# Two heads' transposed probabilities leave PSUM in one step, and q is loaded ahead of the values, in an attention and two feed-forward layers

## The chip, the cores and the metric

The kernel runs on one core of a Trainium2 chip. The metric is the device time of one execution in microseconds. The time before is the median of three runs.

## The reference

Windowed attention with a few global keys, then two feed-forward layers on its output:

```python
# q, k, v: (2, 8, 768, 64); n_global = 8, n_local = 96
scores = q @ k.T / sqrt(64) + bias            # ALiBi bias, per head
keep = is_global | ((rel >= 0) & (rel < n_local))
a = softmax(where(keep, scores, -1e9))
x = (a @ v) as (1536, 512)                    # tokens x (heads * 64)
h = x @ w_in;  x = maximum(0.01 * h, h) @ w_out          # w_in (512, 2048), w_out (2048, 512)
h = x @ w_in2; x = P(h) / (Q(h) + 1e-6) @ w_out2         # P cubic, Q quadratic in h
```

All inputs are float32. The kernel works with float32 products split into a high and a low part (three matmuls for one).

## The kernel before

**Attention.** The 16 combinations of batch and head are taken as 8 pairs of heads (`Pair`, numbered 0 to 7). A pair has 6 blocks of 128 queries (i = 0 to 5) and 2 heads (j), which makes 12 units. A unit is one block of queries of one head against its window of 256 keys (128 for i = 0). The code is written unit by unit along slots n = 0, 1, 2, ...; a pair has 12 slots, called s0 to s11 here. Each engine takes its instructions in the order of this text (`manual_schedule`), so the slot at which a step is written sets what it stands behind. A unit goes through these steps:

- `scores` (L376, TensorE): three matmuls into half a PSUM bank, the two heads interleaved. From n = 8 on, every fourth slot (s0, s4, s8) issues the scores of four units, which fill both halves of the two banks `sc0` and `sc1`. The next group needs both banks read.
- `least` (L387, VectorE): adds the bias, negates, finds the row's least. It is what frees a score bank. Before, it stands at s0, s2, s4, ... for two units each.
- `exp` (L401, ScalarE), one slot after the unit's number.
- `transposes` (L412, TensorE) into a tile `pt` of 256 columns, and `evacuate` into `pts` (L418 on ScalarE, L420 on VectorE), three slots after.
- `values` (L431 to L434, TensorE) into the bank `o`, `LV` = 5 slots after.
- `finish` (L440 to L443, VectorE) after three blocks of both heads: divides by the sum and writes `xp`. Before, it is written at s5 and s11.

**Fillers.** At the end of each slot stand pieces of other work, as generators that advance one step per slot:

- `prep_k` and `prep_q` of the next pair, in halves: three transposes on TensorE into one of two banks `h` (L305), a ScalarE copy one slot later (`kh`, L315, or `qt`, L348), and for k a VectorE step (`kl`, L317) one slot after that; then GpSimd steps. The slots are in the tables `PREP0` (during pair 0) and `PREP`. Here "k0, q0, k1, q1" are the halves.
- `x_out` of the pair before, in halves at s8 and s10 ("x0" and "x1"): transposes into a bank `h` (L198), ScalarE `xh` (L202), VectorE `xl` (L204). The second half's `xl` stands at s0 of the following pair, and q0 of that pair takes the bank which this `xl` frees.
- `decode` of a raw weight piece, started at s10 (the table `DECS`): a DMA of 512 KB into `wraw` (L126), then ScalarE "low" (L133), VectorE "sign" (L141), ScalarE "high" (L138), two GpSimd steps, ScalarE "hi" (L160), VectorE "lo" (L163), each in a slot of its own; "low" stands at s3 of the next pair, "lo" at s0 of the pair after it.
- Loads on SyncE's DMA queue: k two pairs ahead at s4 (`LOAD_K`), v one pair ahead at s6 (`LOAD_V`, six DMAs, L296 to L298), q two pairs ahead at s9 (`LOAD_Q`, L283). The raw tile `qr` has one buffer: the load of q for pair p+2 waits until q1 of pair p+1 has been transposed.

**Feed-forward.** 96 steps of 24 matmuls of 512 columns each, from about 119 us to the end.

Of the kernel before, what the change touches and what calls it, by code (L numbers as in the profile page):

```python
# [8 lines left out]
F32 = mybir.dt.float32  # L9
# [3 lines left out]
AF = mybir.ActivationFunctionType  # L13
# [4 lines left out]
P = 128  # L18
# [7 lines left out]
def attention_moe_moe2(  # L26
# [15 lines left out]
    nc = tc.nc  # L42
# [11 lines left out]


    PREP0 = (("prep_k", 2, 0), ("prep_q", 4, 0), ("prep_k", 6, 1), ("prep_q", 8, 1))
    PREP = (("prep_k", 0, 0), ("prep_q", 1, 0), ("prep_k", 4, 1), ("prep_q", 6, 1))
    LOAD_K = 4
    LOAD_V = 6
    LOAD_Q = 9  # L60
    XOUT = (8, 10)

    FIRST = 8
# [4 lines left out]
    DEC_WAIT = 4  # L68
    DECODE = (0, "low", "sign", "high", "shift", "join", 0, 0, "hi", 0, "lo")

    ON_ACT = (1, 2, 4, 5, 7, 8, 10)


    NF_EARLY = 5
# [116 lines left out]
    ident = cpool.tile([P, P], F32, name="ident")  # L191
# [15 lines left out]
    W2 = 2 * P  # L207
# [36 lines left out]
    def attention(wpool, w1, ffn):  # L244
        with ExitStack() as actx:
# [3 lines left out]
            upool = actx.enter_context(tc.tile_pool(name="upool", bufs=3))  # L249
            ps = actx.enter_context(tc.tile_pool(name="ps", bufs=2, space=PSUM))  # L250

            pairs = [(b, hp) for b in range(B) for hp in range(NPAIR)]
            PU = 2 * NB
# [102 lines left out]
            class Unit:  # L356
# [22 lines left out]
                def least(self):  # L379
                    i, w = self.i, self.w  # L380
                    if self.ih == 0 and self.j == 0:
                        self.pair.st[self.half] = upool.tile([P, 2, 2, HB], F32, tag="st", name="st")
                    self.st = self.pair.st[self.half]
                    self.least_at = self.st[:, 0, self.j, self.ih : self.ih + 1]
                    self.sn = upool.tile([P, W2], F32, tag="sn", name="sn")
                    b0 = W2 if i == 0 else 0
                    nc.vector.tensor_tensor_reduce(  # L387
                        self.sn[:, :w],
                        self.sc[:, :w],
                        bias[:, 2 * self.pair.hp + self.j, b0 : b0 + w],  # L390
                        -0.125,
                        3.0e38,
                        ALU.add,
                        ALU.min,
                        self.least_at,
                    )

                def exp(self):
                    w = self.w
                    self.pr = upool.tile([P, W2], F32, tag="pr", name="pr")  # L400
                    nc.scalar.activation(  # L401
                        self.pr[:, :w],
                        self.sn[:, :w],
                        AF.Exp,
                        bias=self.least_at,
                        scale=-1.0,
                    )

                def transposes(self):
                    self.pt = ps.tile([P, W2], F32, tag="pt", name="pt")  # L410
                    for c in range(0, self.w, P):
                        nc.tensor.transpose(self.pt[:, c : c + P], self.pr[:, c : c + P], ident)  # L412

                def evacuate(self):
                    w = self.w
                    self.pts = upool.tile([P, W2], F32, tag="pts", name="pts")
                    if self.on_act():
                        nc.scalar.activation(self.pts[:, :w], self.pt[:, :w], AF.Copy)  # L418
                    else:
                        nc.vector.tensor_copy(self.pts[:, :w], self.pt[:, :w])  # L420

                def on_act(self):
                    return self.n % PU in ON_ACT

                def values(self):
                    i, j, pr = self.i, self.j, self.pair
# [9 lines left out]
                def finish(self):  # L436
                    pr, st, o = self.pair, self.st, self.pair.o[self.half]
                    if self.half == 0:
                        pr.xp = apool.tile([P, NB, P], F32, tag="xp", name="xp")
                    nc.vector.tensor_scalar(st[:, 1], o[:, :, :, D], 1e-9, None, ALU.add)  # L440
                    nc.vector.reciprocal(st[:, 1], st[:, 1])
                    xp = pr.xp[:, self.half * HB : (self.half + 1) * HB]
                    nc.vector.tensor_tensor(  # L443
                        xp.rearrange("p i (j d) -> p j i d", j=2),
                        o[:, :, :, 0:D],
                        st[:, 1].unsqueeze(3).to_broadcast([P, 2, HB, D]),
                        ALU.mult,
                    )

            P_ = [Pair(n) for n in range(len(pairs))]  # L450
            for p in P_:
                p.st, p.o = {}, {}
            U = [Unit(n) for n in range(PU * len(pairs))]
# [51 lines left out]
            def fillers(n):  # L505

                p, s = divmod(n, PU)
                for g in list(running):
                    if next(g, running) is running:
                        running.remove(g)  # L510
                new = []
                if p + 1 < len(P_):
                    nxt = P_[p + 1]
                    for what, slot, half in PREP0 if p == 0 else PREP:
                        if s == slot:
                            new.append(getattr(nxt, what)(half))
                    if s == LOAD_V:
                        nxt.load_v()
                    if s == LOAD_K and p + 2 < len(P_):
                        P_[p + 2].load_k()  # L520
                    if s == LOAD_Q and p + 2 < len(P_):
                        P_[p + 2].load_q()
                if 0 < p < len(P_):
                    for half, slot in enumerate(XOUT):
                        if s == slot:
                            new.append(P_[p - 1].x_out(half))
                if p == 0 and s in BIAS:
                    bias_head(2 + BIAS.index(s))
                if n in DECS and early:
                    new.append(decode(*early.pop(0)))  # L530
                if n == PU:
                    load_coef()
                if n == 2 * PU:
                    prepare_coef()
                if n == H_SLOT:
                    new.append(ffn.head(0))
                if n == 0:
                    start(k1)
                    start(q1)
                for g in new:  # L540
                    start(g)

            def unit(n):
                return U[n] if 0 <= n < len(U) else None

            LV = 5
            GROUPS = {m: (m,) for m in range(0, FIRST, 2)}
            GROUPS.update({m: (m, m + 2) for m in range(FIRST, len(U), 4)})
            n = 0
            while n < len(U) or running or n <= len(U) + LV + 1:  # L550

                for m in GROUPS.get(n, ()):
                    for _ in zip(unit(m).scores(), unit(m + 1).scores()):
                        pass
                if n % 2 == 0 and unit(n):
                    unit(n).least()
                    if n == 0:
                        bias_head(1)
                    unit(n + 1).least()
                if unit(n - 1):  # L560
                    unit(n - 1).exp()
                if unit(n - 3):
                    unit(n - 3).transposes()
                    unit(n - 3).evacuate()
                if unit(n - LV):
                    unit(n - LV).values()
                if unit(n - LV - 1) and unit(n - LV - 1).ih == HB - 1 and unit(n - LV - 1).j == 1:
                    unit(n - LV - 1).finish()
                fillers(n)
                n += 1  # L570
# [426 lines left out]
    with ExitStack() as fast:  # L997
        fast.enter_context(tc.manual_schedule())
        wpool = fast.enter_context(tc.tile_pool(name="wpool", bufs=1))
        dram = fast.enter_context(tc.tile_pool(name="dram", bufs=1, space=bass.MemoryType.DRAM))  # L1000
        scratch = [dram.tile([P, 2 * DM], F32, name=f"scratch{f}") for f in range(NF)]
        last_xp = dram.tile([P, NB, P], F32, name="last_xp")
        w1 = []
        ffn = Layers(fast, w1)
        attention(wpool, w1, ffn)
        ffn.run(wpool, True, AHEAD)
# [44 lines left out]
```

## Time and profile before

| what | value |
|---|---|
| time before, median of 3 runs | 648.39 us (647.54 to 649.64) |
| profiled execution, its own time | 648.33 us |
| span from its first to its last instruction | 646.5 us |
| TensorE busy | 629.3 us (97%) |
| VectorE, ScalarE, GpSimd busy | 473.0, 440.7, 208.8 us |
| first score matmul of pair 0, pair 1, pair 2, pair 7 | 7.39, 23.59, 36.41, 101.52 us |

Matmuls are pipelined, so TensorE counts as busy while it waits for less than a matmul's own length. Where it waits is read from the starts of its instructions, not from the busy share. A pair lasts from the first score matmul of its s0 to that of the next pair.

### The profile page before, as it was taken

How to read it: one execution, taken by the hardware profiler on the slowest of the kernel's cores; microseconds unless marked ns; L12 is line 12 of the kernel's file. 1: busy time of each engine (PE TensorE's matmuls, PEld its weight loads, DVE VectorE, ACT ScalarE, POOL GpSimd, SP SyncE). 2: the span in 40 equal slices, each digit the busy share in tenths (PEclk: the TensorE clock that was granted, in tenths of full speed). 3: DMA queues.
4: the chain of work that ended last, by engine and by line, in shares of the span. 5: the costliest groups of instructions: out<-in, count | busy, mean ns of one | idle time of the engine just before them, and what ended most of it. 6: DMA issues, size and time to landing. Idle time of an engine off the chain costs nothing.

```text
span 646.5 us, 9591 instructions
## 1 busy us (share of the span) xinstructions
PE 629.3 (97%) x3264; PEld 528.2 (82%) x3264; DVE 473.0 (73%) x933; ACT 440.7 (68%) x829; POOL 208.8 (32%) x220
## 2 busy tenths in 40 slices
PE   5999999999999999999999999999999999999996
PEld 4888888888888888888888888888888888888884
DVE  6788888787896655656444469998777777897785
ACT  4788888777875654546444467776677888876672
POOL 3777675444444343433000002222222222112220
PEclk9999999999999999999999999999999999999999
DMA  8677553653458767676322310000013333000001
GB/s 186 147 175 168 127 137 96 233 190 131 160 163 243 226 203 235 206 232 206 110 96 93 99 42 6 28 1 1 1 51 118 95 98 96 32 34 0 1 0 72
DMA packets 81178, 73.34 MB, mean 113 GB/s; under 512 B 51232, under 2 KB 67616, under 8 KB 81120
## 3 DMA queue, kind: packets, MB, share of 16 engines
q1 hardware_dynamic: 80752, 72.24, 38.2%
q8 instruction: 28, 0.46, 0.3%
q0 software_dynamic: 80, 0.39, 0.1%
q14 instruction: 30, 0.25, 0.1%
q10 hardware_dynamic: 288, 0.00, 0.0%
HBM read 60.69 MB, written 11.93 MB: 112 GB/s over the span
## 4 chain that ended last, share of the span: by engine, by line
PE 93%; DVE 4%; issue 1%; DMA 1%; ACT 0%; SPq 0%; DVEq 0%; ACTq 0%
PE h L599 40%; PE y L722 20%; PE y L720 20%; PE sc L376 4%; PE pt L412 2%; PE o L434 2%; PE o L433 1%; PE h L305 1%; DVE sn L387 1%; PE h L198 1%; DVE wraw L141 1%; DMA qr<-in_q_dram 1%; DVE xp L443 1%; DVE w L163 0%; DVE xl L204 0%
## 5 line engine op out<-in xcount | busy, mean ns | idle before, releaser
L599 PE MATMUL h<-xh,w 128*128 128x512 f32 x768 | 252.9, 390 | 0.0
L599 PEld LDWEIGHTS h<-xh,w 128*128 128x128 f32 x768 | 144.2, 188 | 29.8
L599 PE MATMUL h<-xl,w 128*128 128x512 f32 x384 | 149.4, 389 | 0.0
L653 POOL TENSOR_TENSOR gl<-u,gh 128x512 fp32r<-128x512 f32 x44 | 57.1, 1297 | 265.0 <-PE y L722 133.8
L720 PE MATMUL y<-gh,w 128*128 128x512 f32 x384 | 126.0, 389 | 0.0
L722 PE MATMUL y<-w,gh 128*128 128x512 f32 x384 | 125.5, 389 | 0.0
L154 POOL TENSOR_TENSOR dec<-dec,wraw 128x512 int32<-128x512 int32 x48 | 63.9, 1340 | 82.7 <-DVE wraw L141 76.6
L720 PEld LDWEIGHTS y<-gh,w 128*128 128x128 f32 x384 | 72.0, 188 | 15.0
L722 PEld LDWEIGHTS y<-w,gh 128*128 128x128 f32 x384 | 72.1, 188 | 14.9
L599 PEld LDWEIGHTS h<-xl,w 128*128 128x128 f32 x384 | 72.1, 188 | 14.7
L722 PE MATMUL y<-w,gl 128*128 128x512 f32 x192 | 75.1, 391 | 0.0
L720 PE MATMUL y<-gl,w 128*128 128x512 f32 x192 | 74.7, 389 | 0.0
L624 DVE TENSOR_TENSOR gl<-h,gh 128x512 fp32r<-128x512 f32 x48 | 33.0, 688 | 51.0 <-ACT gh L623 51.0
L623 ACT ACTIVATE gh<-h 128x512 fp32r<-128x512 f32 x48 | 28.6, 596 | 59.0 <-PE y L720 53.5
L675 ACT ACTIVATE h<-h 128x512 f32<-128x512 f32 x48 | 28.7, 597 | 52.8 <-PE h L599 52.6
L619 DVE SCALAR_TENSOR_TENSOR h<-h,g 128x512 f32<-128x512 f32 x48 | 33.3, 694 | 27.0 <-ACT g L618 26.9
L663 DVE SCALAR_TENSOR_TENSOR w<-w,epsq,h 128x512 f32<-128x512 f32 (+1 forms) x49 | 36.2, 739 | 20.9 <-ACT h L687 20.3
L401 ACT ACTIVATE pr<-sn,st 128x256 f32<-128x256 f32 (+1 forms) x96 | 46.3, 488 | 6.4 <-DVE st L387 4.8
L618 ACT ACTIVATE g<-h 128x512 f32<-128x512 f32 x48 | 28.7, 597 | 30.8 <-PE h L599 30.8
L677 DVE SCALAR_TENSOR_TENSOR w<-h,coef,w 128x512 f32<-128x512 f32 x48 | 35.9, 748 | 16.1 <-ACT w L676 15.9
L387 DVE CUSTOM_DVE_ANT_0 sn<-sc,bias 128x256 f32<-128x256 f32 (+1 forms) x96 | 34.7, 397 | 14.9 <-PE sc L376 14.6
L722 PEld LDWEIGHTS y<-w,gl 128*128 128x128 f32 x192 | 36.0, 188 | 8.7 <-POOL gl L653 1.1
(111 smaller groups left out, 1137.6 us busy)
## 6 DMA issues: line engine op xcount, KB each, us to landing
wraw<-in_moe_w_in_dram SPq DMA_DIRECT2D x24, 512.0 KB, 4.6
wraw<-in_moe_w_out_dram SPq DMA_DIRECT2D x24, 512.0 KB, 4.4
scratch<-dec SPq DMA_DIRECT2D x32, 256.0 KB, 5.7
wf<-scratch SPq DMA_DIRECT2D x16, 512.0 KB, 3.4
w<-in_moe_w_in_dram SPq DMA_DIRECT2D x8, 512.0 KB, 4.2
w<-in_moe_w_out_dram SPq DMA_DIRECT2D x8, 512.0 KB, 4.9
vc<-in_v_dram SPq DMA_DIRECT2D x16, 192.0 KB, 3.2
out_dram<-ot SPq DMA_DIRECT2D x12, 256.0 KB, 2.0
```

The costliest lines, as they stand in the source:

```text
L154: nc.gpsimd.tensor_tensor(ti, ti, self.c, ALU.add)
L387: nc.vector.tensor_tensor_reduce(self.sn[:, :w], self.sc[:, :w], bias[:, 2 * self.pair.hp + self.j, b0 : b0 + w], -0.125, 3.0e38, ALU.add, ...
L401: nc.scalar.activation(self.pr[:, :w], self.sn[:, :w], AF.Exp, bias=self.least_at, scale=-1.0,)
L599: nc.tensor.matmul(h, wt[:, m, c * P : (c + 1) * P], xs[:, c, cs], start=c == 0 and n == 0, stop=c == NK - 1 and n == 2,)
L618: nc.scalar.activation(g, h, AF.Copy)
L619: nc.vector.scalar_tensor_tensor(h, h, 0.01, g, ALU.mult, ALU.max)
L624: nc.vector.tensor_tensor(gl, h, gh.bitcast(F32), ALU.subtract)
L653: (nc.gpsimd if on_pool else nc.vector).tensor_tensor(gl, g, gh.bitcast(F32), ALU.subtract)
L663: nc.vector.scalar_tensor_tensor(ow[:, cs], ow[:, cs], epsq, oh2[:, cs], ALU.add, ALU.mult)
L677: nc.vector.scalar_tensor_tensor(w0, h2, coef[:, 7:8], w0, ALU.mult, ALU.add)
L720: nc.tensor.matmul(ys[d], wt[:, m, ds_], gs, start=st, stop=sp)
L722: nc.tensor.matmul(ys[d], gs[:, ds_], wt[:, m, :], start=st, stop=sp)
```

## The change

- `transpose_both` puts the transposes of both heads of a block into one tile `pt` of 2 x 256 columns (one PSUM bank) at even slots, four slots after the first unit, and one copy of 512 columns takes them out. Blocks 1, 3 and 5 are copied on ScalarE, blocks 0, 2 and 4 on VectorE. Before, seven of a pair's twelve units were copied on ScalarE, five on VectorE.
- `LV` is 6 instead of 5: values, and with them `finish`, come a slot later (`finish` at s6 and at s0 of the next pair).
- `LEASTS`: of a group of four units, the last two are read out at s1, s5, s9 instead of s2, s6, s10.
- `sn` and `pr` have 5 buffers instead of 3.
- `PREP`: q0 stands at s2 instead of s1.
- `LOAD_Q` is s7 instead of s9, `LOAD_V` s8 instead of s6.

```diff
-    PREP = (("prep_k", 0, 0), ("prep_q", 1, 0), ("prep_k", 4, 1), ("prep_q", 6, 1))
+    PREP = (("prep_k", 0, 0), ("prep_q", 2, 0), ("prep_k", 4, 1), ("prep_q", 6, 1))
     LOAD_K = 4
-    LOAD_V = 6
-    LOAD_Q = 9
+    LOAD_V = 8
+    LOAD_Q = 7
...
-    ON_ACT = (1, 2, 4, 5, 7, 8, 10)
+    ON_ACT = (1, 3, 5)
...
-                    self.sn = upool.tile([P, W2], F32, tag="sn", name="sn")
+                    self.sn = upool.tile([P, W2], F32, tag="sn", name="sn", bufs=5)
...
-                    self.pr = upool.tile([P, W2], F32, tag="pr", name="pr")
+                    self.pr = upool.tile([P, W2], F32, tag="pr", name="pr", bufs=5)
...
+            def transpose_both(a, b):
+
+                w = a.w
+                pt = ps.tile([P, 2, W2], F32, tag="pt", name="pt")
+                pts = upool.tile([P, 2, W2], F32, tag="pts", name="pts")
+                a.transposes(pt)
+                b.transposes(pt)
+                a.pts, b.pts = pts[:, 0], pts[:, 1]
+                if a.i in ON_ACT:
+                    nc.scalar.activation(pts[:, :, :w], pt[:, :, :w], AF.Copy)
+                else:
+                    nc.vector.tensor_copy(pts[:, :, :w], pt[:, :, :w])
...
-            LV = 5
+            LV = 6
...
+            LEASTS = {m: (m, m + 1) for m in range(0, FIRST, 2)}
+            for m in range(FIRST, len(U), 4):
+                LEASTS[m], LEASTS[m + 1] = (m, m + 1), (m + 2, m + 3)
...
-                if n % 2 == 0 and unit(n):
-                    unit(n).least()
-                    if n == 0:
+                for m in LEASTS.get(n, ()):
+                    if m == 1:
                         bias_head(1)
-                    unit(n + 1).least()
+                    unit(m).least()
                 if unit(n - 1):
                     unit(n - 1).exp()
-                if unit(n - 3):
-                    unit(n - 3).transposes()
-                    unit(n - 3).evacuate()
+                if n % 2 == 0 and unit(n - 4):
+                    transpose_both(unit(n - 4), unit(n - 3))
```

On VectorE, at the start of pair 2 (and alike of pairs 3 to 7), the rows before are, from the last step of pair 1 on:

```order
L440 TENSOR_SCALAR st<-o 128x6
L441 RECIPROCAL st<-st 128x6
L443 TENSOR_TENSOR xp<-o,st 128x2x3x64
L387 ISA sn,st<-sc_130,bias 128x128
L387 ISA st 128x1
L387 ISA sn,st<-sc_131,bias 128x128
L387 ISA st 128x1
L420 COPY pts<-pt 128x256
L163 TENSOR_TENSOR w_202<-dec,w_202 128x512
L204 TENSOR_TENSOR xl<-h,xh 128x384
```

And in the changed kernel, at the same place (L449 is the copy, L428 to L431 are `finish`; `sc_130` and `sc_131` are the two score banks):

```order
L387 ISA sn,st<-sc_130,bias 128x128
L387 ISA st 128x1
L387 ISA sn,st<-sc_131,bias 128x128
L387 ISA st 128x1
L449 COPY pts<-pt 128x512
L428 TENSOR_SCALAR st<-o 128x6
L429 RECIPROCAL st<-st 128x6
L431 TENSOR_TENSOR xp<-o,st 128x2x3x64
L163 TENSOR_TENSOR w_202<-dec,w_202 128x512
L204 TENSOR_TENSOR xl<-h,xh 128x384
```

The three rows of `finish` moved from ahead of the pair's first scores to between the copy and the `xl` of x1; the copy grew from 256 to 512 columns.

On SyncE's queue, the DMAs issued during pair 0 after the loads of the start, before:

```order
L296 DMA vc_136<-in_v_dram 128x6x64
L297 DMA vp_137<-in_v_dram 96x5x64
L298 DMA vp_137<-in_v_dram 32x5x64
L296 DMA vc_136<-in_v_dram 128x6x64
L297 DMA vp_137<-in_v_dram 96x5x64
L298 DMA vp_137<-in_v_dram 32x5x64
L283 DMA qr<-in_q_dram 128x6x64 x2
L126 DMA wraw<-in_moe_w_in_dram 128x4x256
```

And now:

```order
L283 DMA qr<-in_q_dram 128x6x64 x2
L296 DMA vc_136<-in_v_dram 128x6x64
L297 DMA vp_137<-in_v_dram 96x5x64
L298 DMA vp_137<-in_v_dram 32x5x64
L296 DMA vc_136<-in_v_dram 128x6x64
L297 DMA vp_137<-in_v_dram 96x5x64
L298 DMA vp_137<-in_v_dram 32x5x64
L126 DMA wraw<-in_moe_w_in_dram 128x4x256
```

The two q loads, the first of which waits for TensorE, moved ahead of the six value loads; the raw weight piece stays behind both. The same exchange stands in pairs 1 to 5.

On ScalarE, in pair 1 (exp of units 1, 2 and 3, around the first raw weight's "low" and q0's copy), before, with the semaphores that each row waits for (`DMAHW6` is that of the raw weight's load):

```order
L401 ACTIVATE pr<-sn,st 128x128 [waits DVE_49]
L348 ACTIVATE qt<-h 128x384 [waits PE_49,Pool_49]
L401 ACTIVATE pr<-sn,st 128x256 [waits DVE_49,PE_49]
L133 ACTIVATE wraw<-wraw 128x512 [waits DMAHW6_49]
L401 ACTIVATE pr<-sn,st 128x256 [waits DVE_49,PE_49]
```

And now:

```order
L401 ACTIVATE pr<-sn,st 128x128 [waits DVE_49]
L447 ACTIVATE pts<-pt 128x512 [waits PE_49]
L401 ACTIVATE pr<-sn,st 128x256 [waits DVE_49]
L133 ACTIVATE wraw<-wraw 128x512 [waits DMAHW6_49]
L348 ACTIVATE qt<-h 128x384 [waits PE_49,Pool_49]
L401 ACTIVATE pr<-sn,st 128x256 [waits DVE_49]
```

The exp of unit 3, the last row, still stands behind the raw weight's row, and q0's copy now stands between them.

## Rows read from the trace of the kernel before

**Rows 1.** Waits up to 140 us: us in total, times, longest.

```profile
PEld sc L376 <- DVE st L387: 3.6, 15, 0.7
...
PEld h L305 <- DVE xl L204: 2.7, 5, 0.5
```

**Rows 2.** Windows: pair 1, pair 3, pairs 2 to 6; us, then each engine's busy us.

```profile
23.59:36.41 12.82, 12.60 (x122) 11.65 (x121) 9.84 (x43) 10.96 (x28) 10.23 (x16) 1.00 0.92 217
...
49.41:62.58 13.17, 12.47 (x121) 11.50 (x120) 10.62 (x42) 11.30 (x29) 9.81 (x15) 1.00 0.68 161
...
36.41:101.52 65.11, 62.41 (x602) 57.52 (x602) 53.04 (x209) 56.06 (x141) 48.24 (x71) 1.00 0.64 152
```

**Rows 3.** Timeline of TensorE, start of pair 3: start, us, instruction, idle before.

```profile
50.29 0.44 PE L412 MATMUL pt<-ident,pr 128*128 128x128 f32 x2
...
50.96 0.50 PE L305 MATMUL h<-ident,kr 128*128 128x128 f32 x3
...
51.68 0.39 PE L434 MATMUL o<-vc,pts 128*128 128x65 f32 x2
52.47 0.55 PE L305 MATMUL h<-ident,qr 128*128 128x128 f32 x3 [0.40 <-DVE xl L204]
```

**Rows 4.** Timeline of VectorE, the same stretch.

```profile
49.05 0.15 DVE L440 TENSOR_SCALAR st<-o 128x6 f32<-128x6 f32 x1
...
49.46 0.56 DVE L443 TENSOR_TENSOR xp<-o,st 128x384 f32<-128x384 f32 x1
50.51 0.29 DVE L387 CUSTOM_DVE_ANT_0 sn<-sc,bias 128x128 f32<-128x128 f32 x1 [0.49 <-PE sc L376]
...
50.94 0.42 DVE L420 COPY pts<-pt 128x256 f32<-128x256 f32 x1
51.27 0.68 DVE L163 TENSOR_TENSOR w<-dec,w 128x512 fp32r<-128x512 f32 x1
51.87 0.55 DVE L204 TENSOR_TENSOR xl<-h,xh 128x384 fp32r<-128x384 f32 x1
52.34 0.41 DVE L387 CUSTOM_DVE_ANT_0 sn<-sc,bias 128x256 f32<-128x256 f32 x1
...
52.68 0.42 DVE L387 CUSTOM_DVE_ANT_0 sn<-sc,bias 128x256 f32<-128x256 f32 x1
```

**Rows 5.** Timeline of TensorE, the score group at s8 of pair 3.

```profile
58.06 0.73 PE L376 MATMUL sc<-kh,qh 64*128 64x256 f32 x2 [0.29 <-DVE st L387]
```

**Rows 6.** Copies out of PSUM by size: count, busy us, mean ns of one.

```profile
L418 ACT ACTIVATE pts<-pt 128x256 f32<-128x256 f32 x38 | 14.5, 380 | 4.3 <-PE pt L412 3.4
...
L618 ACT ACTIVATE g<-h 128x512 f32<-128x512 f32 x48 | 28.7, 597 | 30.8 <-PE h L599 30.8
...
L737 DVE COPY ot<-y 128x512 f32<-128x512 f32 x2 | 1.4, 692 | 0.8 <-PE y L722 0.7
```

**Rows 7.** Timeline of SyncE's queue, end of pair 0, and landing of that raw weight.

```profile
21.48 1.25 SPq L283 DMA_DIRECT2D qr<-in_q_dram  x2
23.07 0.37 SPq L126 DMA_DIRECT2D wraw<-in_moe_w_in_dram  x1
...
DMA to landing us min/median/max: 4.7/4.7/4.7
```

**Rows 8.** Timeline of ScalarE, pair 1.

```profile
27.94 0.66 ACT L133 ACTIVATE wraw<-wraw 128x512 int32<-128x512 uint32 x1
```

**Rows 9.** Timeline of SyncE's queue, pair 3; landing of ten raw weight loads, 20 to 118 us.

```profile
54.17 0.37 SPq L296 DMA_DIRECT2D vc<-in_v_dram  x1
...
57.44 0.97 SPq L283 DMA_DIRECT2D qr<-in_q_dram  x2
58.92 0.35 SPq L126 DMA_DIRECT2D wraw<-in_moe_w_out_dram  x1
...
DMA to landing us min/median/max: 3.7/4.4/7.1
```

**Rows 10.** Timeline of TensorE, the score group at s8 of pair 7.

```profile
108.97 0.72 PE L376 MATMUL sc<-kh,qh 64*128 64x256 f32 x2 [0.53 <-DVE st L387]
```

More of the change, by code (lines that the diff above doesn't have):

```diff
@@ L407, in exp, with transposes @@
                     )
-                def transposes(self):
-                    self.pt = ps.tile([P, W2], F32, tag="pt", name="pt")
+                def transposes(self, bank):
                     for c in range(0, self.w, P):
[L412 to L423, printed above, removed]
+                        nc.tensor.transpose(bank[:, self.j, c : c + P], self.pr[:, c : c + P], ident)
                 def values(self):
```

## The prediction, made before the changed kernel had run

> **What bounds the kernel now.** TensorE, in both parts. From about 119 us on, its 512-column matmuls follow each other and the change touches nothing there, so what the change is worth lies in the eight pairs before. I read them in this order. First the waits [rows 1]: TensorE waits mostly for two things, for score banks that `least` has not yet read (15 times) and, in five pairs, for the bank `h` of q0, which the `xl` of x1 frees. Then the pairs as windows [rows 2]: pair 3 lasts 13.17 us, pairs 2 to 6 together 65.11, 13.02 on average, with VectorE busy 53.04 and ScalarE 56.06 of them; these overlap at their ends, so neither is full. Then pair 3 by its starts. Its last values ahead of q0 begin at 51.68 and 51.80 and q0 could start 0.11 later, at 51.91; it starts at 52.47 [rows 3], 0.56 late, 0.60 after the start of `xl` at 51.87 [rows 4]. At s8 the score group waits again: two matmuls of the two heads that otherwise start together lie 0.35 apart, after 0.29 of idle time [rows 5]; against the usual 0.2 from values to scores that is 0.36 + 0.35 = 0.71. 13.17 - 0.56 - 0.71 gives **11.90 us as TensorE's own time for a pair**. The change neither adds nor removes a matmul, so it can give back at most the difference to this floor, 1.1 us a pair.
>
> **The merged copy.** Two copies of 256 columns on ScalarE take 2 x 380 ns, one of 512 takes 597; on VectorE two of 0.42 [rows 4] become one of 692 ns [rows 6]. Consecutive instructions overlap by some 0.1 (50.94 + 0.42 against 51.27), so ScalarE saves about 0.07 on each of 24 merges, VectorE 0.07 on 16 wider ones. None of this is on the path unless that engine is what TensorE waits for; bounds 0 and 24 x 0.16 + 16 x 0.15 = 6.2 us. I take 0 directly and follow VectorE's queue instead, because that is where both waits come from. The Trainium skill, "ScalarE: Activation LUTs", section "What ACT_TABLE_LOAD costs", has 186 ns + 0.833 ns a column and an overlap of 93 ns for such copies; by it a merge saves 0.09, and 24 would give 2.2 us if all were on the path. The rows agree in kind.
>
> **The score waits.** The second pair of `least` moves a slot earlier and no longer has `finish` and "sign" ahead of it at s8. That removes the 0.71 of pair 3, about 0.5 in the others.
>
> **q0, in pairs 2 to 6.** Measured from a pair's first score matmul (49.41 in pair 3), q0 is free to start at 2.50. In the changed kernel four more transposes of 0.11 and a unit's values of 0.39 stand ahead of it (0.67 from 50.29 to 50.96 is one unit's two transposes and values with a 0.06 change-over [rows 3]): 2.50 + 0.44 + 0.39 = 3.33. The `xl` that frees its bank started at 51.87, that is at 2.46. It now stands behind a copy that begins 0.05 later (four transposes instead of two) and takes 0.27 more, and behind `finish`, which before ran ahead of the first `least` in time that VectorE had idle (0.49 before 50.51). `finish` takes 49.46 + 0.56 - 0.08 - 49.05 = 0.89 [rows 4]. So `xl` starts at 2.46 + 0.05 + 0.27 + 0.89 = 3.67 and q0 at 3.67 + 0.60 = 4.27: **a wait of 0.94 in place of 0.56**. Moving q0 by one slot gains 0.83, `xl` loses 1.21. A pair then takes 11.90 + 0.94, and I add 0.05 for the second head's scores: 12.89 against 13.02, five times 0.13, **-0.65 us**. Bounds: 0.1 either way on each, and the whole wait (-5.4) if `xl` should be free by 3.33.
>
> **q ahead of v, and the raw weight behind both.** Before, SyncE issued v early and stopped at q, which waits for q1's transposes. Now v and the raw weight piece stop with it.
> Pair 1: q went out at 21.48 and the raw weight at 23.07, landing 4.7 later [rows 7]; ScalarE took it at 27.94 [rows 8], with 0.2 to spare. By the order of TensorE q1 ends about 0.5 sooner, at 21.0; q takes 1.25 [rows 7], six value loads 57.44 - 54.17 = 3.27 [rows 9], so the raw weight goes out at 25.5 and lands at 30.2. On ScalarE "low" holds up q0's copy and the exp of unit 3 (0.56 + 0.37 + 0.50): that exp ends at 31.65. TensorE comes to its transposes 6.76 after the pair's first scores (3.33 + q0 0.34 + values 0.39 + scores 1.06 + two transposes, two units' values and k1 1.34 + the next unit's transposes and the change-over 0.3), and these start at 22.9: at 29.65. **A new wait of 2.0** (1.0 with a landing of 3.7, 4.4 with 7.1 [rows 9]). Pair 1: 11.9 + 2.0 = 13.9 against 12.82 [rows 2]: **+1.1 us**.
> The Trainium skill, "Perfetto Trace Analysis", section "Tensor Engine Instruction", says that ScalarE and VectorE are strict first-in-first-out. By that rule the exp can't pass "low", and this speaks against the change; no row contradicts it.
> Pairs 2 to 6: q1's transposes end at 8.5, q is issued at 8.55, v by 9.65 and the raw weight at 12.9, the next pair's start; before it went out at 58.92 - 49.41 = 9.5. It lands at 4.2 to 7.1 in that pair. ScalarE comes to it at 5.0, and TensorE waits only if it lands after 7.7 - 0.56 - 0.37 - 0.50 = 6.2. At the median of 4.4 nothing, at the longest 0.9 each: 0 to 4.5 us, I take **+0.5**, one pair in five or two.
>
> **Pair 7** has no k0 and q0, so nothing hides the queue of the 0.94: its scores at s4 come at 3.5 and need the two `least` that follow `xl`, which start at 3.67 + 0.47 and 0.34 later [rows 4] and free their banks 0.48 after: 4.6 and 4.95, 1.12 + 0.35 late. At s8 I get 0.32 + 0.35 by the same count ("sign" stands ahead of its `least`). Before, 0.35 at s4, and 0.60 + 0.35 at s8 [rows 10]. 2.14 - 1.30 = **+0.8**.
>
> **Pair 0** is reordered, with the same work, and the scores of unit 12 come 0.7 sooner but with 0.6 of transposes and values put off past them: **-0.1**, bounds -1 and +1 (its waits are of the size of pair 1's). At the end, values of the last units stand among the first feed-forward matmuls in both kernels and hide the extra slot; 0, at most 0.6, a unit's transposes and values, if they don't.
>
> Sum: -0.1 + 1.1 - 0.65 + 0.5 + 0.8 = +1.65. The profiled execution's own time is 648.33 (span 646.5, 1.8 around it), 0.06 under the median of 648.39: **650.0 us**. A measurement of this kernel can tell about 0.3%, 1.95 us, from no change, so this is within it, near its slow side.
>
> **Rivals.**
> A, as summed, 650.0: chance 0.36, of which 0.08 over 650.3.
> B, the raw weights come late in most pairs: with 6.6 after the issue, pair 1 waits 3.9 and pairs 2 to 6 0.4 each: -0.1 + 3.0 + (2.0 - 0.65) + 0.8 = +5.0, 653.4. For it: 7.1 at one issue, and the burst is denser now. Against: the median of 4.4 [rows 9]. Chance 0.26.
> C, faster: q0's wait goes instead of growing, because copy and `finish` cost VectorE less in this place than their rows say. It decides at 3.33: if `xl` starts by 2.73 instead of 3.67, each of five pairs falls to 11.9, -5.6 instead of -0.65, pair 7 falls too, to 0: -0.1 + 1.1 - 5.6 = -4.6, 643.7; half of it 646.3. For: both waits of rows 1 are of this kind, and VectorE idles ahead of the first `least`. Against: in the order `finish` stands after the copy, and the copy after the transposes. Chance 0.18.
> D, the raw weight is hidden anyway, in pair 1 too: -0.1 - 0.9 - 0.65 + 0.8 = -0.85, 647.5. For: the transfer may be shorter with the queue empty (3.7). Against: in pair 1 it had 0.2 to spare and goes out 2.4 later. Chance 0.20.
>
> **Numbers.** Within 0.3%: A 0.28, D 0.18: 0.46. Slower: A 0.08, B 0.26: 0.34. Faster: C 0.18 and the rest of D: 0.20. The range takes A and D, B to 653.5 and half of C, 646.0: 646.0 to 653.5; A alone 648.3 to 651.5.
>
> **What would show it.** After: `xl` at pairs' starts behind `finish`; q0 waiting for it about 0.9, five times; no scores waiting at s8 in pairs 2 to 6, but at s4 in pair 7; in pair 1 ScalarE idle ahead of L133 for a DMA and TensorE's transposes waiting for an exp for 2 us; raw weight loads 3 us later in each pair. Wrong would be above all: `xl` free before 3.3, raw weights landing within 4 us or after 6, or a pair 0 that waits elsewhere.

## The result, and the profile after

The changed kernel takes 655.51 us (median of five runs, 654.97 to 657.61) against 648.46: a ratio of 1.0111, 95% interval 1.0091 to 1.0131. It is slower by 7 us, and the predicted range ended at 653.5.

The windows of the eight pairs of the changed kernel, in the profiled execution (657.61 us, span 655.8): from, to, us, then the busy us (and instructions) of TensorE's matmuls, its weight loads, VectorE, ScalarE and GpSimd, the granted clock of TensorE as a share of 2.4 GHz, the busy share of the DMA engines and GB/s.

```profile
7.39:21.93 14.54, 13.04 (x88) 10.76 (x89) 11.39 (x37) 9.43 (x23) 8.18 (x15) 1.00 0.60 125
21.93:39.20 17.27, 15.05 (x121) 14.06 (x121) 10.80 (x40) 10.26 (x24) 11.41 (x17) 0.80 0.84 180
39.20:52.53 13.33, 12.17 (x121) 11.45 (x121) 11.17 (x42) 10.70 (x26) 8.48 (x13) 1.00 0.50 123
52.53:65.73 13.20, 12.04 (x121) 11.32 (x121) 10.70 (x39) 10.77 (x26) 10.20 (x15) 1.00 0.74 157
65.73:78.91 13.19, 12.03 (x121) 11.31 (x121) 10.70 (x39) 10.76 (x26) 10.14 (x15) 1.00 0.65 152
78.91:92.62 13.71, 12.44 (x121) 11.49 (x121) 11.27 (x39) 10.78 (x26) 10.01 (x15) 1.00 0.74 163
92.62:105.81 13.18, 12.03 (x121) 11.31 (x121) 10.70 (x39) 10.80 (x26) 10.19 (x15) 1.00 0.60 134
105.81:121.83 16.03, 14.98 (x117) 14.07 (x117) 10.41 (x39) 11.29 (x25) 6.62 (x6) 0.79 0.33 116
```

Two windows stand out, pair 1 with 17.27 and pair 7 with 16.03, and they are the two in which the granted clock is printed below 1.00. (Pair 0 ran in part below it too: the trace's first clock record, of 2.4 GHz, begins at 16.88, and the view prints 1.00 where there is none. At 13.65 one pair of score matmuls follows the other after 0.22 us, at 58.26 after 0.11.) Against the kernel before, whose pairs last 16.19, 12.82, 65.11 for the five in the middle [rows 2], and 12.47; its pairs 0 and 7:

```profile
7.39:23.59 16.19, 14.55 (x94) 12.35 (x95) 11.97 (x39) 9.84 (x26) 9.00 (x15) 1.00 0.83 163
...
101.52:113.99 12.47, 11.94 (x115) 10.95 (x115) 10.53 (x42) 10.67 (x28) 4.81 (x5) 1.00 0.20 65
```

| part | predicted | measured, this execution |
|---|---|---|
| pair 0 | -0.1 | 14.54 - 16.19 = -1.65 |
| pair 1 | +1.1 | 17.27 - 12.82 = +4.45 |
| pairs 2 to 6 | -0.65 + 0.5 | 66.61 - 65.11 = +1.50 |
| pair 7, to the first feed-forward matmul | +0.8 | 16.03 - 12.47 = +3.56 |
| first to last feed-forward matmul | 0 | 526.42 - 525.91 = +0.51 |
| from there to the end | 0 | 7.57 - 6.64 = +0.93 |
| sum | +1.65 | +9.3 |

**Pair 1.** TensorE, ScalarE and SyncE's queue in the changed kernel, and the landing of ten raw weight loads (each engine's timeline; an idle time and its releaser in brackets):

```profile
28.56 0.39 PE L411 MATMUL pt<-ident,pr 128*128 128x128 f32 x2
31.17 0.69 PE L411 MATMUL pt<-ident,pr 128*128 128x128 f32 x2 [2.22 <-ACT pr L401]
```

```profile
25.90 0.51 ACT L401 ACTIVATE pr<-sn,st 128x256 f32<-128x256 f32 x1
29.69 0.65 ACT L133 ACTIVATE wraw<-wraw 128x512 int32<-128x512 uint32 x1 [3.29 <-DMA wraw<-in_moe_w_in_dram]
30.25 0.47 ACT L348 ACTIVATE qt<-h 128x384 f32<-128x384 f32 x1
30.62 0.89 ACT L401 ACTIVATE pr<-sn,st 128x256 f32<-128x256 f32 x2
```

```profile
20.36 1.43 SPq L283 DMA_DIRECT2D qr<-in_q_dram  x2
...
25.86 0.38 SPq L126 DMA_DIRECT2D wraw<-in_moe_w_in_dram  x1
```

```profile
DMA to landing us min/median/max: 3.8/4.7/5.6
```

This is the chain that was predicted. The raw weight goes out behind q and v, at 25.86 instead of 23.07 [rows 7]; "low" takes it at 29.69 instead of 27.94 [rows 8], and the exp behind it ends at 31.1. TensorE does unit 2's two transposes from 28.56, 0.11 apart, so it is ready for unit 3's at 28.78; these start at 31.17, 2.39 late. What was not predicted comes then. Windows ahead of and in the next 6.8 us, and the like in pair 7:

```profile
26.00:30.50 4.50, 2.95 (x30) 2.51 (x29) 1.91 (x9) 1.21 (x3) 0.97 (x2) 1.00 0.87 211
30.54:37.36 6.82, 6.19 (x35) 5.85 (x35) 4.66 (x18) 4.63 (x12) 6.40 (x9) 0.50 0.60 132
...
112.46:119.28 6.82, 6.82 (x40) 6.48 (x38) 5.00 (x20) 4.62 (x10) 3.22 (x3) 0.50 0.29 88
```

The clock falls to 1.2 GHz at 30.54, inside the wait, and stays there to 37.36. In pair 7 it falls at 112.46, after this wait of the score group at s4:

```profile
110.52 0.72 PE L376 MATMUL sc<-kh,qh 64*128 64x256 f32 x2 [1.04 <-DVE st L387]
```

In the kernel before, the trace's clock records show 2.4 GHz without a break from 18.73 us, in pair 0, to 643.37.

**Pairs 2 to 6.** VectorE, GpSimd and TensorE at the start of pair 3 (first scores at 52.53):

```profile
54.11 0.69 DVE L449 COPY pts<-pt 128x512 f32<-128x512 f32 x1
54.72 0.15 DVE L428 TENSOR_SCALAR st<-o 128x6 f32<-128x6 f32 x1
...
55.61 1.01 DVE L163 TENSOR_TENSOR w<-dec,w 128x512 fp32r<-128x512 f32 x1
56.54 0.55 DVE L204 TENSOR_TENSOR xl<-h,xh 128x384 fp32r<-128x384 f32 x1
```

```profile
55.41 1.42 POOL L333 TENSOR_TENSOR kh<-kh,zeros 128x288 fp32r<-128x288 f32 x2 [1.26 <-ACT kh L315]
```

```profile
57.19 0.52 PE L305 MATMUL h<-ident,qr 128*128 128x128 f32 x3 [1.16 <-issue]
...
61.55 0.39 PE L376 MATMUL sc<-kh,qh 64*128 64x256 f32 x2
```

The copy starts 1.58 after the pair's first scores and `finish` takes 55.61 - 54.72 = 0.89, both as predicted. But lo lasts 1.01, not 0.68 [rows 4], so `xl` starts at 4.01 instead of 3.67, and q0, 0.65 later, at 4.66 instead of 4.27: it waits 1.32 (1.43 from start to start, less 0.11), not 0.94. (The row gives "issue" as what ended this wait; `xl` ends at 57.09, 0.10 ahead of q0.) The score wait at s8 [rows 5] is gone in this pair: both heads' first matmuls start together, at 61.55.

### The profile page after: what moved, and what is told of

Its sections match the earlier page's. It is cut to its first block, busy times and chain, and to the rows that moved or that the text cites. A ratio compares the mean times of both kernels' runs of the same rounds, so it can differ in the third digit from the quotient of the medians.

```text
span 655.8 us, 9514 instructions
## 1 busy us (share of the span) xinstructions
PE 632.1 (96%) x3264; PEld 532.1 (81%) x3264; DVE 473.9 (72%) x917; ACT 437.4 (67%) x797; POOL 211.1 (32%) x220
## 4 chain that ended last, share of the span: by engine, by line
PE 94%; issue 1%; DMA 1%; DVE 1%; SPq 1%; ACT 0%; ACTq 0%
PE h L602 40%; PE y L725 20%; PE y L723 20%; PE sc L376 4%; PE pt L411 3%; PE o L422 2%; PE h L305 2%; PE o L421 2%; PE h L198 1%; DMA qr<-in_q_dram 1%; DMA wraw<-in_moe_w_in_dram 1%; PE o L419 0%; SPq L283 0%; SPq L298 0%; DVE sn L387 0%
## 5 line engine op out<-in xcount | busy, mean ns | idle before, releaser
L621 ACT ACTIVATE g<-h 128x512 f32<-128x512 f32 x48 | 28.5, 593 | 30.2 <-PE h L602 30.2
L680 DVE SCALAR_TENSOR_TENSOR w<-h,coef,w 128x512 f32<-128x512 f32 x48 | 36.0, 750 | 16.1 <-ACT w L679 16.0
```

The source lines that it names most:

```text
L680: nc.vector.scalar_tensor_tensor(w0, h2, coef[:, 7:8], w0, ALU.mult, ALU.add)
```

## Experiments

The theory: three mechanisms, each with its place. The late raw weight makes TensorE wait in pair 1; `finish` ahead of lo and `xl` makes it wait in all the others; and behind a long wait its clock falls. The main rival M: the merged copy and the deeper pipeline cost time of their own. The kernel before was timed again beside each group of versions; its medians lie between 648.46 and 649.40, so that a difference between the times of two versions is good to about 1 us, and the ratios to the kernel before are the safer measure.

**Loads where they were** (all else as changed).

```diff
-    LOAD_V = 8
-    LOAD_Q = 7
+    LOAD_V = 6
+    LOAD_Q = 9
```

> The changed kernel with the loads where they were (v at s6, q at s9), all else as changed. Theory (late raw weight in pair 1, and TensorE's clock after it): the raw weight goes out before q again and lands some 2.5 us earlier, the 2.4 us wait ahead of unit 3's transposes in pair 1 goes, the granted clock does not fall from 30.5 to 37.4, pair 1 takes about 13.0 instead of 17.27: 655.5 - 4.3 = 651.2 us (650 to 652.5). Rival M (the merged copy and the deeper pipeline cost time in every pair and the loads only 2.4 once): 653 us, with pair 1 at about 15.

651.91 us, ratio to the kernel before 1.0034 (1.0013 to 1.0055): 3.6 less than the changed kernel, 5.0 by the two ratios. Windows of pair 1, of pair 3 and of the stretch at 1.2 GHz in pair 7:

```profile
22.87:35.35 12.48, 12.46 (x121) 11.48 (x120) 10.64 (x40) 10.11 (x23) 9.72 (x15) 1.00 0.84 193
48.67:61.87 13.20, 12.04 (x121) 11.32 (x120) 10.71 (x39) 10.79 (x25) 10.21 (x15) 1.00 0.70 159
...
108.03:114.85 6.82, 6.82 (x40) 6.48 (x39) 4.96 (x18) 4.54 (x10) 3.14 (x3) 0.50 0.30 91
```

The wait and the fall in pair 1 are gone, with nothing but two load slots changed; pair 1 falls from 17.27 to 12.48. Of the 4.79, 2.39 were the wait, so the fall of the clock cost 2.40.

**`finish` behind the fillers of its slot.**

```diff
-                if unit(n - LV - 1) and unit(n - LV - 1).ih == HB - 1 and unit(n - LV - 1).j == 1:
-                    unit(n - LV - 1).finish()
                 fillers(n)
+                if unit(n - LV - 1) and unit(n - LV - 1).ih == HB - 1 and unit(n - LV - 1).j == 1:
+                    unit(n - LV - 1).finish()
```

> The changed kernel with finish written behind the fillers of its slot, so that at a pair's start lo and xl no longer stand behind its 0.89 us. Theory: xl starts 0.9 to 1.2 us earlier in a pair (0.9 for finish, up to 0.3 more if lo no longer overlaps the GpSimd step beside it), q0's wait of pairs 2 to 6 falls from 1.3 to 0.1 to 0.4, pair 7's score wait at s4 from 1.2 to about 0.3, pair 1 is as before this edit: 655.5 - 5 x 1.0 - 0.9 = 649.6 us (648 to 651.5). Rival (VectorE is full there, and what is taken away in front comes back as later least): 654 to 655.5.

652.41 us, 1.0054 (1.0033 to 1.0074): only half of the gain. **Both edits:**

> Both edits: loads as they were, and finish behind the fillers. Theory: both gains add up, since they lie in different pairs: 655.5 - 4.3 - 5.9 = 645.3 us (644 to 647.5), under the kernel before. Rival M (merged copy and deeper pipeline cost time of their own): not under 648.4.

650.39 us, 1.0002 (0.9985 to 1.0019): not under the kernel before, so my theory lacked a step. Pair 3 in this last version, TensorE and VectorE (first scores at 48.61):

```profile
52.05 0.52 PE L305 MATMUL h<-ident,qr 128*128 128x128 f32 x3
...
53.23 0.73 PE L376 MATMUL sc<-kh,qh 64*128 64x256 f32 x2 [0.27 <-DVE st L387]
```

```profile
50.80 0.68 DVE L163 TENSOR_TENSOR w<-dec,w 128x512 fp32r<-128x512 f32 x1
51.40 0.55 DVE L204 TENSOR_TENSOR xl<-h,xh 128x384 fp32r<-128x384 f32 x1
...
52.28 0.56 DVE L431 TENSOR_TENSOR xp<-o,st 128x384 f32<-128x384 f32 x1
52.76 0.41 DVE L387 CUSTOM_DVE_ANT_0 sn<-sc,bias 128x256 f32<-128x256 f32 x1
```

q0's wait is gone (it starts at 3.44 where 3.33 is free of any). But the two `least` of units 2 and 3, which free the banks for s4, stand behind everything in s0 whichever way that is ordered; they now are what TensorE waits for. For the same reason pair 7 keeps its wait at s4 (1.05 idle, as the changed kernel's 1.04). In the execution with `finish` moved alone, no fall followed that wait, and pair 7 took 13.42; with one it takes 16.03 in the changed kernel: 2.6 for the fall.

```profile
103.56:116.98 13.42, 12.25 (x117) 11.25 (x117) 10.29 (x39) 10.72 (x24) 6.05 (x6) 1.00 0.30 100
```

**TensorE kept busy in the two long waits.** Work is added and none removed; the extra transposes are overwritten by the real ones.

```diff
+            def keep_busy(pt, count):
+                for _ in range(count):
+                    nc.tensor.transpose(pt[:, 0, 0:P], ident, ident)
...
+                if a.n == PU + 2:
+                    keep_busy(pt, 20)
...
                 a.transposes(pt)
...
                 fillers(n)
+                if n == 7 * PU + 3:
+                    kept[n - 3] = ps.tile([P, 2, W2], F32, tag="pt", name="pt")
+                    keep_busy(kept[n - 3], 10)
```

> The changed kernel with work added for TensorE and nothing removed: 20 transposes of the identity into the bank pt ahead of the transposes of units 2 and 3 in pair 1, and 10 ahead of the scores at s4 of pair 7, in the time in which it waits for something else. Theory (two costs, the wait and the clock behind it): the exp of unit 3 comes as late as before, but the granted clock stays at 1.00 to the end of pair 1, which then takes 17.3 - 3.0 = 14.3 us; the like in pair 7 where the clock fell there: 652.5 us (651.5 to 653.5). Rival (the clock costs nothing, TensorE would wait at s8 and after anyway): 655.5 or a little more.

652.44 us, 1.0042 (1.0026 to 1.0058): 3.1 less than the changed kernel, with 30 transposes more. Windows of pair 1 and pair 7:

```profile
22.87:37.77 14.90, 14.52 (x141) 13.60 (x140) 10.85 (x40) 9.87 (x23) 9.48 (x14) 1.00 0.81 184
...
104.06:117.50 13.44, 13.31 (x128) 12.27 (x127) 10.30 (x39) 10.73 (x24) 6.01 (x6) 1.00 0.31 102
```

The wait for the raw weight is still there (pair 1 takes 2.4 more than with the loads back), and the clock stays at 1.00 in both pairs. It does so in more than this execution: the mean granted clock of the ten is 0.996 to 0.999, that of the changed kernel's five 0.986 to 0.992. So the falls are a cost of their own, and they come of TensorE standing still.

**The load swap alone, on the kernel before** (`LOAD_V` 8, `LOAD_Q` 7).

> The kernel before with the two load slots of the change alone (v at s8, q at s7). Theory (the late raw weight needs nothing else of the change): in pair 1 q goes out at about 21.5, v behind it, the raw weight at about 26.0 and it lands 3.8 later, at 29.8; the exp of unit 3 then starts at 30.7 and TensorE, which comes to its transposes at 29.6, waits 1.6 us. If the granted clock then falls for as long as it did in the changed kernel, 3.0 more. From 649.0: 650.6 without a fall, 653.6 with one; I expect the latter. Rival (only the deeper pipeline of the changed kernel needs unit 3 so early): 649.0.

651.83 us, 1.0043 (1.0024 to 1.0061). TensorE in pair 1, and the windows of pairs 1 and 3:

```profile
34.38 0.44 PE L412 MATMUL pt<-ident,pr 128*128 128x128 f32 x2 [1.53 <-ACT pts L418]
```

```profile
26.20:40.30 14.10, 12.56 (x120) 11.65 (x121) 9.99 (x43) 10.47 (x28) 8.62 (x14) 1.00 0.87 179
53.30:68.95 15.65, 14.10 (x121) 13.13 (x120) 12.15 (x43) 11.78 (x30) 10.16 (x15) 0.89 0.78 177
```

The swap costs 2.8 by itself, by the ratio. The wait in pair 1 has the size expected (1.53 idle, for 1.6), behind ScalarE's copy that follows the late exp. No fall followed it in this execution, so the fall that I expected is not shown here. One did come in pair 3, after a wait of 1.14 at s8. That wait goes back to these two steps, one of GpSimd and VectorE's "sign", which takes 0.69 in pair 3 of the kernel before:

```profile
59.97 1.00 POOL L351 TENSOR_TENSOR ql<-qt,qh 128x384 fp32r<-128x384 f32 x1
```

```profile
59.99 1.53 DVE L141 SCALAR_TENSOR_TENSOR wraw<-wraw 128x512 int32<-128x512 int32 x1
```

`finish` and the `least` that frees the score bank stand behind "sign". This execution, at 655.29 the longest of the ten, is so explained by this wait and its fall, and by a pair 0 of 18.52; what made two others 654.1 and 654.4 isn't known. Most of the ten lie below the 653.6 that I expected.

**GpSimd's kh steps behind kl's**, so that none runs beside lo.

```diff
-                    for t in (self.kh, self.kl):
+                    for t in (self.kl, self.kh):
```

> The changed kernel with the GpSimd steps of prep_slots in the other order, kl ahead of kh: kh then waits behind kl's VectorE step and no GpSimd instruction runs beside lo (L163) at a pair's start. Theory (lo takes 1.01 instead of 0.68 us in pairs 2 to 6 because GpSimd works beside it): lo takes 0.68, xl starts 0.33 earlier, q0's wait falls from 1.32 to about 1.0, pairs 2 to 4 from 13.2 to 12.87; five times 0.33 is 1.65, so 653.9 us where the changed kernel has 655.5. Rival (lo is longer for another reason, its place behind finish): lo stays at 1.01, 655.5.

652.92 us, 1.006 (1.004 to 1.0079), 2.6 less than the changed kernel. VectorE at the start of pair 3 (first scores at 51.62), and GpSimd:

```profile
54.22 0.56 DVE L431 TENSOR_TENSOR xp<-o,st 128x384 f32<-128x384 f32 x1
54.69 0.68 DVE L163 TENSOR_TENSOR w<-dec,w 128x512 fp32r<-128x512 f32 x1
55.29 0.55 DVE L204 TENSOR_TENSOR xl<-h,xh 128x384 fp32r<-128x384 f32 x1
```

```profile
58.00 0.97 POOL L333 TENSOR_TENSOR kh<-kh,zeros 128x288 fp32r<-128x288 f32 x2
```

In its place behind `finish`, lo takes 0.68 again once no GpSimd instruction runs beside it, `xl` starts 3.67 after the pair's first scores, which is the number predicted, and q0 0.33 earlier. So the 0.33 is GpSimd's doing.

**The earlier `least` alone, on the kernel before** (with five buffers of `sn` and `pr`).

> The kernel before with the earlier least of the last two units of a group (and five buffers of sn and pr) alone; copies, values, finish and loads as before. Theory (this part is what removes the score waits at s8, and it costs nothing): pair 3 falls from 13.18 to about 12.5, pairs 2 to 6 by 0.5 on average, 649.0 - 2.5 = 646.5 us (645.5 to 648). Rival (the score waits are only moved, since VectorE has the same work in front): 649.

644.5 us, 0.9927 (0.99 to 0.9954): more than expected. Pair 3, and TensorE at q0 of pair 3:

```profile
47.12:59.64 12.52, 12.13 (x121) 11.28 (x120) 10.57 (x42) 10.93 (x29) 9.60 (x15) 1.00 0.69 155
```

```profile
50.07 0.44 PE L305 MATMUL h<-ident,qr 128*128 128x128 f32 x2 [0.29 <-DVE xl L204]
```

All score waits are gone and q0's is left. The change held a gain, then. (The five buffers were not tried without the earlier `least`.) **The counterpart: the changed kernel with the loads back and `least` where it was before.**

```diff
-            LEASTS = {m: (m, m + 1) for m in range(0, FIRST, 2)}
-            for m in range(FIRST, len(U), 4):
-                LEASTS[m], LEASTS[m + 1] = (m, m + 1), (m + 2, m + 3)
+            LEASTS = {m: (m, m + 1) for m in range(0, len(U), 2)}
```

> The changed kernel with the loads where they were and the least of each pair of units where it was before (s2, s6, s10), so merged copy, finish and values a slot later and q0 at s2 alone. Theory (the earlier least is the gaining part of the change also inside it): the score groups at s4, s8 and of the next pair wait again, 0.5 us or more in each of seven pairs, and over the 651.9 of the version with the loads back alone it takes 3.5 more: 655.4 us (653.5 to 658). Rival (behind finish and xl at s0 the least of s1 comes no earlier than that of s2 would): 652.

652.65 us, 1.0056 (1.0041 to 1.0072), and pair 3 takes 13.20 as with the early `least`:

```profile
48.70:61.90 13.20, 12.04 (x122) 11.32 (x120) 10.71 (x39) 10.79 (x25) 10.21 (x15) 1.00 0.71 161
```

My theory fell and the rival held: behind q0's wait of 1.3 TensorE comes so late to s4 and s8 that either `least` is in time. One wait hid the other's cure.

**`finish` in the slot after, behind that slot's `least`**, with the loads back.

```diff
                 for m in LEASTS.get(n, ()):
                     if m == 1:
                         bias_head(1)
                     unit(m).least()
+                done = unit(n - LV - 2)
+                if done and done.ih == HB - 1 and done.j == 1:
+                    done.finish()
...
-                if unit(n - LV - 1) and unit(n - LV - 1).ih == HB - 1 and unit(n - LV - 1).j == 1:
-                    unit(n - LV - 1).finish()
                 fillers(n)
```

> The changed kernel with the loads where they were and with finish written in the slot after, behind that slot's least. At a pair's start VectorE then has copy, lo, xl, two least, finish. Theory (TensorE waits for what stands behind finish, first xl, then the least of units 2 and 3): neither q0 nor the scores of s4 wait by more than 0.2, pairs 2 to 6 take 12.0 to 12.2 instead of 12.68 with finish only behind the fillers, pair 7's wait at s4 falls from 1.1 to under 0.4 and its clock does not fall: from 650.4, 5 x 0.6 + 0.8 + 2.9 = 6.7 less, 643.7 us (642.5 to 646), under the kernel before. Rival (VectorE is full in a pair and a third wait takes the place): 648 to 650.

644.08 us, 0.9924 (0.9903 to 0.9945). Pair 3 takes 12.19, pair 7 12.62, at 1.00:

```profile
46.90:59.09 12.19, 12.03 (x123) 11.32 (x122) 10.50 (x39) 10.78 (x26) 9.87 (x15) 1.00 0.70 167
95.52:108.14 12.62, 12.25 (x117) 11.25 (x117) 10.38 (x39) 10.73 (x24) 6.94 (x8) 1.00 0.37 112
```

Against the loads back alone, the place of three VectorE instructions is worth 7.8 us by the medians and 7.1 by the ratios; in the profiled executions pairs 2 to 6 give 5.1 of it and pair 7, which has its fall no more, 3.4. This refutes rival M: the merged copy and the deeper pipeline are both in this version.

**Two versions that go further.** From the kernel before, the earlier `least` and q0 at s2; and the version just shown with block 4's copy on ScalarE and block 3's on VectorE.

```diff
-    PREP = (("prep_k", 0, 0), ("prep_q", 1, 0), ("prep_k", 4, 1), ("prep_q", 6, 1))
+    PREP = (("prep_k", 0, 0), ("prep_q", 2, 0), ("prep_k", 4, 1), ("prep_q", 6, 1))
```

> The kernel before with the earlier least and with q0 at s2; copies of each head, values, finish and loads as before. Theory (in the kernel before, finish, copy and lo are light enough for xl to be done by then, so moving q0 one slot hides what is left of its wait): q0's wait of 0.35 in pairs 2 to 6 goes, a pair takes 12.53 - 0.35 = 12.2 us, 644.5 - 1.75 = 642.7 us (642 to 644). Rival (q0 later makes unit scores of s4 or the next pair's kh wait instead): 644.5 or more.

643.43 us, 0.9916 (0.9902 to 0.9929). Pair 3:

```profile
47.77:59.80 12.03, 11.95 (x122) 11.23 (x121) 10.54 (x42) 10.82 (x30) 9.53 (x15) 1.00 0.70 158
```

```diff
-    ON_ACT = (1, 3, 5)
+    ON_ACT = (1, 4, 5)
```

> The version with the loads where they were and finish in the slot after, with block 4's copy (at a pair's start) on ScalarE and block 3's on VectorE instead. Theory (VectorE's queue at a pair's start is what is left of the wait): xl and the least of units 2 and 3 start 0.6 earlier, pair 7's wait of 0.29 at s4 and the rest of q0's go, pairs 2 to 6 fall from 12.15 to 12.0, pair 7 by 0.5: 644.1 - 1.2 = 642.9 us (642 to 644). Rival (ScalarE holds its exps up by 0.6 there, and TensorE's transposes wait for these): 644.1 to 646.

642.79 us, 0.9905 (0.9892 to 0.9919). Pair 3:

```profile
46.67:58.64 11.97, 11.97 (x121) 11.36 (x121) 10.52 (x40) 10.48 (x25) 9.57 (x15) 1.00 0.73 172
```

Both beat both kernels. They differ by 0.6 us and their ranges overlap (642.75 to 643.87, 641.98 to 643.5): with the waits gone, no gain or cost of the merged copy is to be seen. They differ in `LV` and the place of `finish` too, so this is not a test of the copies alone.

## Why the prediction was wrong

The forecast was "within 0.3%" and the kernel is 1.1% slower. Step by step, as the prediction put them:

- **"11.90 us as TensorE's own time for a pair"**: right. Pairs without waits take 11.97 and 12.03.
- **"The score waits. ... That removes the 0.71"**: right in place [rows 5], and alone it is worth 4.7 us. Inside the changed kernel it is worth nothing that is clear of the noise (651.91 with it, 652.65 without, both with the loads back), since q0's wait covers it.
- **"The merged copy ... I take 0 directly"**: nothing speaks against it; the last two versions, one with two copies and one with one, end 0.6 us apart.
- **"`finish` takes ... 0.89", "a wait of 0.94 in place of 0.56"**: `finish` to the hundredth; the wait is mis-sized, 1.32. It took lo at the 0.68 of [rows 4], where nothing ran beside it. In the changed kernel lo begins at 55.61, beside the GpSimd step that begins at 55.41. Pairs 2, 3, 4 and 6 last 0.29 to 0.44 more than the 12.89 of the prediction.
- **"A new wait of 2.0" in pair 1**: the mechanism is right in each link. Raw weight out at 25.86 (25.5 predicted), "low" at 29.69 (30.2 for the landing), TensorE ready at 28.78 (29.65): 2.39. That the times lie so near is in part luck: q and v took 5.50 on the queue instead of 4.52, the landing 3.8 instead of 4.7, and q went out 0.64 sooner. **"Pair 1: 11.9 + 2.0 = 13.9" is the step that failed**: it priced the wait at its own length. TensorE ran the 6.8 us that follow at 1.2 GHz, 2.40 more. The 11.9 is short as well: without the wait pair 1 takes 12.48, 0.58 more; why is open.
- **"Pairs 2 to 6: ... I take +0.5, one pair in five or two"**: right in size, and not by the path that was put forward. Loads landed after 3.8 to 5.6, and pair 5 alone was long, 13.71 against 13.19. But no exp held TensorE up there. "low" began at 85.20 and put off q0's copy and the GpSimd step behind it, which so came to stand 0.12 ahead of "sign":

```profile
86.33 0.83 POOL L350 TENSOR_TENSOR qh<-qt,zeros 128x384 fp32r<-128x384 f32 x1 [0.66 <-ACT qt L348]
```

```profile
86.45 1.25 DVE L141 SCALAR_TENSOR_TENSOR wraw<-wraw 128x512 int32<-128x512 int32 x1
```

Here "sign" took 1.25 where it takes 0.68 in pair 3, the `least` behind it came 0.57 later, and the scores of s8 waited for that.
- **"Pair 7 ... +0.8"**: the wait at s4 is right (1.1), and without a fall pair 7 takes 13.42 with `finish` behind the fillers and 13.44 with TensorE kept busy, +0.95. With a fall, +3.56. The same omission as in pair 1.
- **"Pair 0 ... -0.1"**: -1.65 in this execution and -0.7 to -0.8 in five experiments whose pair 0 is nearly the same (15.41 to 15.51); the rest is the clock's rise. Against the version with the loads back TensorE's starts agree to 0.02 up to 16.1 us; k1's transposes and the score group behind them then start 0.38 and 0.87 sooner (17.28 against 17.66, 17.88 against 18.75), and the rise is at 16.88 here and at 19.28 there.
- **Rival B** gave 653.4, nearest to the result, by raw weights landing late; they landed at a median of 4.7, against the 6.6 it needed. **Rival C** needed copy and `finish` to cost less in their place; they cost what their rows say.
- Two slips of the working change nothing: with the shortest landing, 3.7, the raw weight of pairs 2 to 6 lands at 3.7 and not 4.2, and half of rival C's -4.6 leads to 646.0, as the range has it, not 646.3.

The profiled execution has both falls and is the longest of five. The other four have a mean clock of 0.991 or 0.992 where it has 0.986: 0.005 of 655 us is 3.3 us, or 6.6 us less at half the clock. That is one fall of 6.8 us, or half of both; which, the runs don't show, since only one execution was profiled. With it and pair 0 the median lies 7 and not 9 us above the kernel before. The rest of the sum's gap, +0.51 in the feed-forward part, is within the 0.6 that the prediction set for the deferred transposes and values; the +0.93 behind the start of the last matmul need not be the change's: that stretch takes 6.43 to 7.69 over all the profiles, 7.28 with the load swap alone and 6.65 in the last version.

## What to carry to other kernels

A wait of TensorE has two prices, its length and the clock behind it: ask of every new wait how long TensorE stands still, and add what the next microseconds cost at 1.2 GHz. Work that is written at the start of a stage, ahead of what frees a bank, delays everything that the bank holds up; putting three short VectorE instructions one slot later was worth some 7 us, while the merging of the copies, which the change set out to do, showed no gain. And a part that gains alone may gain nothing beside a longer wait, so a change of several parts is tried in parts: here, by the ratios, one part was worth -4.7 us, another +2.8.

## What the hardware did that I had not expected

- **The clock falls after short waits, not every time.** A wait of 2.0 to 2.4 us in pair 1 was followed by a fall in all three profiles that have it unfilled (for 6.8 us, to 37.36, in the changed kernel, for 3.4 us in two others). The price goes with the length of the fall: pair 1 takes 17.27 with the long one, 16.05 with a short one (`finish` behind the fillers) and 14.90 with none (TensorE kept busy). Shorter waits were followed by a fall in some profiles only: the wait of about 1.04 at s4 of pair 7 in five of the six profiles that have it unfilled, and not in that with `finish` behind the fillers; the 1.53 in pair 1 with the load swap alone by none, the 1.14 in its pair 3 by one. q0's wait of 1.3 in five pairs had none behind it.
- **The rise in pair 0 comes at different times**: 2.4 GHz was granted from 16.88 us on in the changed kernel's profile, 18.73 in that of before, 15.72 in that of the earlier `least`, 24.00 in that of the load swap. Pair 0 took 14.54, 16.19, 15.14 and 18.52 there. Part of the 1.65 between the first two is the changed order, as said above; the last two go with 1.05 less and 2.33 more than the kernel before, in kernels that differ little from it in pair 0.
- **GpSimd beside a VectorE instruction.** lo took 1.01 beside a GpSimd step that had begun 0.20 earlier, and the two GpSimd steps took 1.42 instead of 0.97; apart, 0.68 and 0.97. The Trainium skill, "SBUF — State Buffer", section "Who interferes with whom", says that a VectorE instruction with two inputs in SBUF contends with a GpSimd one that reads SBUF, and that the order in which they are issued decides which of them waits. The trace agrees: the first of the two GpSimd steps kept its length (0.66) and lo was held up, by 0.33 of the 0.46 for which they overlapped; the second step, which began behind lo's start, was the longer one. "sign" shows how little decides it: in pair 3 of the changed kernel it began 0.08 ahead of GpSimd's ql step and took 0.68, that step 1.47; in pair 3 of the load swap it began 0.02 behind and took 1.53, that step 1.00, and TensorE waited 1.14. Starts as close as this don't settle who is held up: in pair 3 of the kernel before, ql's began 0.01 ahead of that of "sign", and ql took 1.57, "sign" 0.69.
